# A gated mix of windowed attention and a token MLP: second x block transposed by DMA, its gate logits on VectorE, and a new order for the first microseconds

## The chip, the cores and the metric

The kernel runs on one core of a Trainium2 chip. A core has TensorE (PE: matrix products, with a separate stream of weight loads, PEld), VectorE (DVE), ScalarE (ACT), GpSimd (POOL) and SyncE (SP), which here issues every DMA. The metric is the device time of one execution in microseconds (us), as the median of several runs.

## The reference

```python
def _A_ref(x, wqkv, wo):            # B, S, D = 1, 2048, 512
    H = 32; Dh = D // H; W = 256
    qkv = (x @ wqkv).reshape(B, S, 3, H, Dh).transpose(2, 0, 3, 1, 4)
    q, k, v = qkv[0], qkv[1], qkv[2]
    scores = jnp.einsum("bhqd,bhkd->bhqk", q, k) * (Dh ** -0.5)
    # a query sees its own and the 255 earlier tokens; the others get -1e9
    p = _softmax(scores, axis=-1)
    o = jnp.einsum("bhqk,bhkd->bhqd", p, v)
    return o.transpose(0, 2, 1, 3).reshape(B, S, D) @ wo

def _B_ref(x, w1, b1, w2, b2):      # F = 1376, over the token axis
    h = _layernorm(x, axis=-1)
    u = _gelu(jnp.einsum("bsd,sf->bdf", h, w1) + b1)
    y = jnp.einsum("bdf,fs->bds", u, w2) + b2
    return y.transpose(0, 2, 1)

g = _sigmoid((x * gate_w).sum(-1, keepdims=True))
return g * _A_ref(x, wqkv, wo) + (1 - g) * _B_ref(x, w1, b1, w2, b2)
```

Both parts read the same x (2048 x 512, bf16). Attention has 32 heads of 16 columns and a window of 256 tokens; the MLP mixes tokens, so its first product needs the normalised x of all 2048 tokens before it can be finished.

## The kernel before, in words

x is cut into four blocks of 512 tokens (16 tiles of 128). x is loaded with tokens on the partitions (`xo`, tasks `x0.0`, `x0.2`, `x1.4`, `x2.8`, `x3.12`), for the statistics (`bs`, `ba`: mean and variance), the normalised copy `h` and the gate logits. For the Q, K and V products a transposed copy is needed (`XT0` to `XT3`). Blocks 0 and 1 are transposed on PE from `xo` (tasks `xta0.*`, `xta1`, `xtb1.*`, line 588), into PSUM, and copied out by ACT or DVE (`xtc`, lines 582 and 583). Blocks 2 and 3 are loaded a second time by a transposing DMA (`xt2`, `xt3`, line 444).

The weights of Q and K come as four loads of 128 rows (`wqk0` to `wqk3`, line 451), those of V in one (`wv`, line 455). A projection is a chain of four products over these rows (`q0_1` is part 0 of Q for block 1; `k`, and `v` by token tile, likewise; `q0_1.0` and `q0_1.2` are its first and second two products). For block 0 the first product of a chain is cut into two halves of 256 columns (`.0`, `.1`), so that it can start with half of the block; `.2` to `.4` are the products with weight rows 1 to 3. All products of these chains, and those of the MLP, stand at line 647.

Scores are made per token tile and group of heads (`s3.A0`, `s3.B1`, `s3.CNone`; lines 919 and 899), each into two pairs of PSUM banks; ACT takes their exp (`e`, line 944); POOL or DVE zeroes what is outside the window (`m`, lines 516, 960, 980); PE multiplies with V (`pv`, line 1005); DVE transposes, divides by the sum and transposes back (`n1`, `n2`, `nz`, `n3`, `n4`). Two corner pieces per tile need V rows on other partitions, which SP copies (`vs`, `vz`). The MLP's first product makes eleven chains `u0` to `u10` of 16 products, which need all 16 `h`; one block of gelu steps on ACT follows; then `y0` to `y15`, eleven products of the MLP and four of the output projection in one bank, are scaled and biased by `f` and stored by `o`.

The gate logits: for blocks 0 and 1 PE multiplies XT with the gate vector (`gate0`, `gate1`, 16 products of one column each, line 779). For blocks 2 and 3 DVE multiplies `xo` with a broadcast copy of the vector (`gw`, line 487) and adds up along the row (`gl8` to `gl15`, line 799). `gatem`, `gatee` and `ez` turn them into factors that the division `nz` uses.

The order on each engine is written out by hand in `PLAN` (from line 190), one list of task names per engine; the digits after a colon are the PSUM banks or buffers that a task takes. Each engine works through its list in order, so a task that waits holds everything behind it. `arrange` (line 85) only merges the five lists; the times given to the tasks serve that merge. `THEN` names score and `pv` tasks after which the products that follow are issued as four products of 32 columns each, in the tile shape of `pv`, instead of one of 128. At the start PE multiplies zeros (`warm`, line 571), 7 times.

Of the kernel before, what the change touches and what calls it, by code (L numbers as in the profile page):

```python
# [84 lines left out]
def arrange(tasks):  # L85
# [21 lines left out]
    while len(order) < len(tasks):  # L107
# [84 lines left out]
        warm:6 xta0.1:37 xta0.0:65 k3_0.0:4 k2_0.0:5 k1_0.0:1 k0_0.0:0 k2_0.1 k0_0.1 q0_0.0:3 q1_0.0:2 q1_0.1  # L192
        k2_0.2 q0_0.1 k1_0.1 q1_0.2 k3_0.1 q0_0.2 k0_0.2 k1_0.2 k3_0.2 xta1:67 xtb1.2 xtb1.3 q1_0.3 k1_0.3 xtb1.1
        q1_0.4 k1_0.4 q0_0.3 xtb1.0 q2_0.0:7 q0_0.4 q2_0.1 q2_0.2 k0_0.3 q2_0.3 k0_0.4 k2_0.3 q2_0.4 k2_0.4 k3_0.3
        q3_0.0:6 s0.A0:02 q3_0.1 q3_0.2 q3_0.3 q3_0.4 q0_1.0:5 k3_0.4 q0_1.2 v3.0:7 s1.B0:02 v3.2 v0.0:6 v0.2
        s1.A1:40 v1.0:7 v1.2 k3_2.0:6 k3_2.2 v5.0:5 biast:4 v5.2 v2.0:7 s1.CNone:20 v2.2 s0.CNone:24 gate0:6
        s-1.CNone:02 k3_1.0:6 k3_1.2 k2_2.0:7 s0.A1:02 k2_2.2 q3_1.0:5 q3_1.2 v12.0:6 v12.2 v14.0:7 v14.2 pv-1.0:0
        s2.B1:42 q1_1.0:6 k2_1.0:7 q1_1.2 k2_1.2 s1.A0:04 pv0.0:2 pv0.1 v15.0:7 pv0.2 v15.2 k0_2.0:6 k0_2.2
        s1.B1:04 v6.0:7 v6.2 v10.0:6 v10.2 s2.A0:20 k1_1.0:7 k1_1.2 v4.0:4 v4.2 v13.0:5 v13.2 pv1.0:2 pv1.1 pv1.2
        pv1.3 s2.B0:60 v7.0:4 v7.2 pv1.4 k0_1.0:5 k0_1.2 v8.0:4 v8.2 s2.A1:06 v11.0:5 v11.2 v9.0:4 s2.CNone:02 v9.2  # L200
        q2_1.0:5 k1_2.0:7 k1_2.2 q2_1.2 u2.0:6 s3.A0:02 u3.0:7 u2.2 u3.2 s3.CNone:40 u3.4 u3.6 gate1:3 u2.4 u3.8
        s4.B1:24 pv2.0:0 pv2.1 pv2.2 pv2.3 u2.6 u3.10 s3.B0:42 u3.12 u3.14 u2.8 u2.10 s3.A1:04 u2.12 u2.14 q0_2.0:7
        s3.B1:02 q0_2.2 u7.0:6 u7.2 u7.4 u7.6 s4.B0:40 pv3.0:2 pv3.1 pv3.2 pv3.3 u7.8 u7.10 s4.A0:04 u7.12 q3_2.0:7
        u7.14 s4.A1:20 q3_2.2 u0.0:6 u0.2 s5.B0:24 u0.4 u0.6 u0.8 u10.0:7 s4.CNone:02 u10.2 u10.4 u0.10 s6.B0:40
        u10.6 u0.12 u10.8 u10.10 u10.12 s5.B1:24 pv4.0:0 pv4.1 pv4.2 pv4.3 u0.14 u10.14 s5.A1:24 u6.0:6 u6.2 u6.4
        s6.A0:20 u6.6 q2_2.0:7 q2_2.2 s5.A0:42 u6.8 u6.10 u6.12 u6.14 s5.CNone:04 k3_3.0:7 k3_3.2 u5.0:6 s6.A1:20
        u5.2 q1_2.0:7 u5.4 q1_2.2 u5.6 s6.B1:24 pv5.0:0 pv5.1 pv5.2 pv5.3 u5.8 u5.10 s7.A0:42 u5.12 u1.0:7 u1.2
        s8.B0:04 u5.14 u1.4 u1.6 s6.CNone:02 k1_3.0:6 u1.8 k1_3.2 s7.B0:40 u1.10 u1.12 u4.0:6 u1.14 u4.2
        s7.CNone:24 pv6.0:0 pv6.1 pv6.2 pv6.3 q0_3.0:7 u4.4 s8.CNone:24 u4.6 q0_3.2 u4.8 s8.B1:02 u4.10 u4.12 u4.14
        s7.B1:40 u9.0:7 u9.2 u8.0:6 u9.4 s7.A1:42 u8.2 u9.6 u9.8 s8.A1:04 u8.4 u9.10 pv7.0:2 pv7.1 u9.12 u8.6  # L210
        s8.A0:04 u9.14 u8.8 u8.10 u8.12 u8.14 s9.B0:40 pv7.2 pv7.3 q1_3.0:7 q2_3.0:5 q2_3.2 pv8.0:0 pv8.1 pv8.2
        q1_3.2 k2_3.0:4 q3_3.0:5 pv8.3 q3_3.2 k0_3.0:6 k0_3.2 y0.0:7 y0.2 k2_3.2 y0.4 y0.6 y4.0:6 s9.B1:20 y0.8
        y4.2 y4.4 y0.10 s9.A0:42 y0.11 y0.13 y4.6 s9.CNone:40 y4.8 y4.10 y4.11 y4.13 s9.A1:42 y8.0:7 y8.2 y7.0:6
        y8.4 s10.B1:40 y7.2 y8.6 y7.4 s13.CNone:24 y7.6 y7.8 y8.8 y8.10 y7.10 s11.CNone:20 y7.11 y8.11 y8.13
        s10.A0:42 y7.13 pv9.0:0 pv9.1 pv9.2 s10.CNone:64 pv9.3 y1.0:3 y1.2 y9.0:2 y1.4 s10.B0:64 y9.2 y1.6 y1.8
# [12 lines left out]
        xtc0.0.1 xtc0.1.0 xtc0.1.1 xtc1.2 xtc1.3 xtc1.1 xtc1.0 kc1_0 kc0_0 kc2_0 e0.A0.0:4 e0.A0.1 kc3_0 e1.B0.0:3
        vc3 vc0 e1.A1.0:1 e1.B0.1 e1.A1.1 vc5 e1.CNone.0:2 e1.CNone.1 e0.CNone.0:0 vc2 e-1.CNone.0:5 gatee0
        e-1.CNone.1 e0.CNone.1 kc3_1 e0.A1.0:6 kc2_2 e0.A1.1 vc12 vc14 e2.B1.0:5 e2.B1.1 kc2_1 e1.A0.0:4 e1.A0.1  # L230
        vc15 kc0_2 e1.B1.0:6 vc6 e1.B1.1 e2.A0.0:0 vc10 e2.A0.1 vc4 vc13 e2.B0.0:4 vc7 e2.B0.1 kc0_1 vc8 e2.A1.0:3
        vc11 e2.A1.1 e2.CNone.0:2 e2.CNone.1 vc9 e3.A0.0:1 e3.A0.1 e3.CNone.0:6 e3.CNone.1 e4.B1.0:7 e4.B1.1
        e3.B0.0:0 gatee1 e3.B0.1 e3.A1.0:4 e3.A1.1 e3.B1.0:3 e3.B1.1 e4.B0.0:2 e4.B0.1 gatee2 e4.A0.0:5 e4.A0.1
        e4.A1.0:1 e4.A1.1 e5.B0.0:6 e5.B0.1 e4.CNone.0:0 e4.CNone.1 e6.B0.0:4 e6.B0.1 gatee3 e5.B1.0:3 e5.B1.1 ub0
        e5.A1.0:2 e5.A1.1 e6.A0.0:0 e6.A0.1 e5.A0.0:5 e5.A0.1 e5.CNone.0:1 e5.CNone.1 e6.A1.0:7 e6.A1.1 e6.B1.0:8
        e6.B1.1 e7.A0.0:2 e7.A0.1 e8.B0.0:3 e8.B0.1 e6.CNone.0:6 e6.CNone.1 e7.B0.0:5 e7.B0.1 e7.CNone.0:1
        e7.CNone.1 e8.CNone.0:0 e8.CNone.1 e8.B1.0:4 e8.B1.1 e7.B1.0:6 e7.B1.1 e7.A1.0:8 e7.A1.1 e8.A1.0:7 e8.A1.1
        e8.A0.0:2 e8.A0.1 e9.B0.0:5 e9.B0.1 gelu e9.B1.0:1 e9.B1.1 e9.A0.0:6 e9.A0.1 e9.CNone.0:7 e9.CNone.1
        e9.A1.0:0 e9.A1.1 e10.B1.0:8 e10.B1.1 e13.CNone.0:2 e13.CNone.1 e11.CNone.0:3 e11.CNone.1 e10.A0.0:4
# [42 lines left out]
def kernel(  # L282
# [996 lines left out]
```

## Time and profile before

| | |
|---|---|
| Median of 5 runs | 206.68 us (206.05 to 207.07) |
| Profiled execution: its time / its span | 206.59 us / 204.9 us |
| Busy: PE, PEld | 196.9 us (96%), 93.3 us (46%) |
| Busy: ACT, DVE, POOL | 170.2 us (83%), 149.7 us (73%), 81.5 us (40%) |
| First product with weights starts / first u product | 6.76 us / 49.77 us |
| Two DMA transposes: SP held, first and second | 7.21 us, 3.65 us |

The span runs from the first to the last instruction. In the timeline a line gives the start in us, the length, engine, line, operation, output<-input, shapes and the count of merged instructions; in brackets stands how long the engine was idle before and what it waited for. In the chain of waits each piece is what the end of the kernel was waiting for at that moment. "SPq" is SyncE's queue: an issue there that takes long holds all later loads. "Issue to landing" counts from the issuing instruction to the last part of the data.

### The profile page before, as it was taken

Reading aid. Unit: us, or ns where it says so; the run is one execution under the profiler, and the core shown is the slowest. Engines: PE = TensorE matmul, PEld = TensorE weight load, DVE = VectorE, ACT = ScalarE, POOL = GpSimd, SP = SyncE. Lnnn points to the kernel's source line nnn. Section 1 sums busy time; section 2 is a strip of 40 time slices with the busy share of each in tenths; the row PEclk is TensorE's granted clock in tenths of the full one; section 3 lists DMA queues with packets and bytes.
Section 4 is the critical chain, followed back from the end, with each engine's and each line's share of the span. In section 5 each row is a group of like instructions: output and inputs, shape, how many; then the busy total and the mean of one; then the engine's idle time right before and its main releaser. Section 6 shows DMA issues by size and latency. Waiting matters only on the chain.

```text
span 204.9 us, 8428 instructions
## 1 busy us (share of the span) xinstructions
PE 196.9 (96%) x3768; PEld 93.3 (46%) x3768; DVE 149.7 (73%) x273; ACT 170.2 (83%) x200; POOL 81.5 (40%) x80
## 2 busy tenths in 40 slices
PE   7899999999999999999999999899999999999993
PEld 3453443343635345453544454334445534553662
DVE  3699889998796836689776689463795865758483
ACT  2379999989978898998889697999897889798831
POOL 8722479634425044004072440009974204400930
PEclk9999999999999999999999999999999999999999
DMA  5998997930040101001059890010103031000201
GB/s 160 347 236 185 248 307 227 352 120 11 3 113 24 31 2 31 3 3 28 3 137 410 317 308 3 18 36 10 52 0 96 17 113 56 11 29 3 80 3 53
DMA packets 21106, 21.45 MB, mean 105 GB/s; under 512 B 5486, under 2 KB 19182, under 8 KB 21070
## 3 DMA queue, kind: packets, MB, share of 16 engines
q1 hardware_dynamic: 21070, 20.92, 33.9%
q8 instruction: 29, 0.48, 1.0%
q14 instruction: 7, 0.06, 0.1%
HBM read 15.61 MB, written 2.10 MB: 86 GB/s over the span
## 4 chain that ended last, share of the span: by engine, by line
PE 85%; DVE 6%; DMA 3%; issue 2%; ACT 1%; SPq 1%; DVEq 0%
PE pb L647 61%; PE ps L1005 11%; PE ps L919 9%; DMA xo<-in_A_x_dram 3%; PE ps L899 3%; DVE ps L1083 2%; DVE zt L1100 1%; ACT et L944 1%; DVE ps L1087 1%; SPq L435 1%; PE pb L588 1%; SPq L451 0%; DVE rd L1091 0%; DVE KT L583 0%; DVE ot L422 0%
## 5 line engine op out<-in xcount | busy, mean ns | idle before, releaser
L944 ACT ACTIVATE et<-ps 128x1024 bf16<-128x1024 f32 (+1 forms) x106 | 99.1, 997 | 12.4 <-PE ps L919 8.3
L516 POOL TENSOR_SCALAR_AFFINE_SELECT et<-et 128x1024 bf16<-128x1024 bf16 (+3 forms) x41 | 54.4, 1336 | 68.2 <-ACT et L944 32.9
L944 ACT ACTIVATE XT<-ps 128x1024 bf16<-128x1024 f32 x48 | 46.5, 1028 | 5.2 <-PE ps L919 4.1
L647 PEld LDWEIGHTS <-wb 128*128 128x128 bf16 (+4 forms) x438 | 31.7, 98 | 36.4 <-issue 5.9
L647 PE MATMUL pb<-h,wb 128*128 128x512 bf16 (+1 forms) x176 | 44.3, 381 | 0.0
L647 PE MATMUL pb<-ug,wb 128*128 128x512 bf16 (+6 forms) x262 | 44.3, 367 | 0.0
L647 PE MATMUL pb<-XT,wqkv 128*128 128x512 bf16 (+1 forms) x136 | 32.9, 368 | 0.5 <-DVE XT L583 0.5
L516 POOL TENSOR_SCALAR_AFFINE_SELECT XT<-XT 128x1024 bf16<-128x1024 bf16 x12 | 13.7, 1145 | 44.6 <-ACT XT L944 38.0
L1083 DVE STREAM_TRANSPOSE ps<-ps 128x1024 f32<-128x1024 f32 (+1 forms) x17 | 20.4, 1202 | 14.7 <-PE ps L1005 14.6
L919 PE MATMUL ps<-QZ,KT 32*128 32x256 bf16 (+1 forms) x528 | 23.9, 262 | 1.7 <-ACT et L944 0.8
L1005 PEld LDWEIGHTS <-VA 128*32 128x32 bf16 (+1 forms) x1056 | 19.4, 97 | 6.0 <-issue 3.6
L422 DVE TENSOR_SCALAR ot<-pb,c,c 128x512 bf16<-128x512 f32 (+1 forms) x15 | 11.6, 774 | 14.0 <-PE pb L647 13.8
L731 DVE TENSOR_TENSOR QZ<-pb,par 128x1024 bf16<-128x1024 f32 x16 | 19.3, 1219 | 1.7 <-PE pb L647 1.4
L919 PEld LDWEIGHTS <-KT 32*128 32x128 bf16 x528 | 8.0, 92 | 25.7 <-ACT et L944 12.7
L647 PEld LDWEIGHTS <-wqkv 128*128 128x128 bf16 x136 | 11.6, 98 | 13.6 <-issue 1.4
L1005 PE MATMUL ps<-et,VA 128*32 128x128 bf16 (+2 forms) x752 | 17.4, 216 | 0.0
L647 PE MATMUL pb<-wo,xo 128*128 128x512 bf16 (+2 forms) x98 | 17.0, 371 | 0.0
L647 PE MATMUL pb<-wqkv,XT 128*128 128x512 bf16 x64 | 16.4, 381 | 0.0
L1005 PEld LDWEIGHTS <-VZ 128*32 128x32 bf16 x832 | 13.2, 98 | 0.0
L747 DVE BATCH_NORM_STATS2 stats<-xo 128x6 f32<-128x512 bf16 x16 | 10.6, 683 | 3.4 <-DMA xo<-in_A_x_dram 3.3
L1100 DVE TENSOR_TENSOR zt<-ps,rd 128x512 bf16<-128x512 f32 (+1 forms) x17 | 11.2, 659 | 0.5
L980 DVE TENSOR_TENSOR et<-et,mask 128x1024 bf16<-128x1024 bf16 x13 | 9.9, 764 | 2.2 <-ACT et L944 2.2
(72 smaller groups left out, 181.6 us busy)
## 6 DMA issues: line engine op xcount, KB each, us to landing
wb<-in_B_w_dram SPq DMA_DIRECT2D x8, 512.0 KB, 5.3
wb<-in_B_w_dram SPq DMA_DIRECT2D x2, 2048.0 KB, 10.6
out_dram<-ot SPq DMA_DIRECT2D x15, 128.0 KB, 1.8
VZ<-VA SPq DMA_DIRECT2D x26, 70.0 KB, 2.1
xo<-in_A_x_dram SPq DMA_DIRECT2D x3, 512.0 KB, 5.6
wb<-in_B_w_dram SPq DMA_DIRECT2D x4, 352.0 KB, 7.1
wqkv<-in_A_wqkv_dram SPq DMA_DIRECT2D x4, 256.0 KB, 6.0
wb<-in_B_w_dram SPq DMA_DIRECT2D x1, 1024.0 KB
```

Source lines behind the costliest of these rows:

```text
L422: return nc.vector.tensor_scalar(out=out_, in0=in_, scalar1=scale, scalar2=bias, op0=ALU.mult, op1=ALU.add)
L516: return nc.gpsimd.affine_select(out=out_, in_=in_, pattern=[[0, n] for n in pattern] + [[step, HB]], compare_op=op, fill=0.0, base=base_, ...
L647: made.append(nc.tensor.matmul(buf(b)[c:z_, c0:c0 + w_], lhsT=lhsT[:, c:z_], rhs=rhs, start=(j == 0), stop=(j == n - 1), skip_group_check= ...
L731: lambda k=k, b=b: nc.vector.tensor_tensor(out=QZ[:, k, :, (i % NQ) * SB:(i % NQ + 1) * SB], in0=buf(b)[:, None, :].to_broadcast([P, 2, SB ...
L747: f"bs{t_}", {"DVE": 0.67}, lambda b=b, t_=t_: nc.vector.bn_stats(buf(b)[:], xo[:, t_, :]),
L899: made.append(nc.tensor.matmul(buf(b2[r // 2])[m_:m_ + HB, at:at + P], lhsT=keys(t_, k)[rows, a:a + HB], rhs=q[rows], start=True, stop=Tru ...
L919: made.append(nc.tensor.matmul(to[:, :, done:done + m], lhsT=keys(t_, k)[rows], rhs=q[rows], start=True, stop=True, tile_position=(32 * r, 0),
L944: lambda n_=n_: nc.scalar.activation(out=shape(buf(e)[:, n_ * 1024:(n_ + 1) * 1024]), in_=shape(buf(b2[n_])), func=ACT.Exp, scale=SCALE),
L980: return nc.vector.tensor_tensor(out=view, in0=view, in1=mask[:, "AB".index(x), None, :].to_broadcast([P, n_, HB]), op=ALU.mult)
L1005: return lambda: nc.tensor.matmul(to(), lhsT=v() if callable(v) else v, rhs=buf(e)[rows, col:col + n], start=first, stop=last, tile_positi ...
L1083: f"n1{j}", {"DVE": 0.10 + 0.53 * f_}, lambda: nc.vector.transpose(out=view(), in_=view()), [last], uses=[o],
L1100: lambda: nc.vector.tensor_tensor(out=buf(zt)[:, 0:w].rearrange("q (k b d) -> q k b d", k=4, d=DH), in0=blocks_of()[:, :, :, 0:DH], in1=bu ...
```

## The change

`NPE` goes from 2 to 1: block 1 is no longer transposed on PE but loaded a second time by a transposing DMA (`xt1`). The gate logits get a count of their own, `NGP = 1`, so block 1's come from DVE (`gl4` to `gl7`), and `gate1` is gone. The four loads of Q and K weight rows stand right behind the first x block on SP. Block 0's transposes are cut into four tasks, one per bank, instead of two. There are 5 products with zeros instead of 7. The task `table`, an exp of one column late in ACT's list, is dropped. All five lists of `PLAN` and the set `THEN` are new, and some of the planner's times. No arithmetic changes except where block 1's logits are summed.

```diff
 PLAN = dict(
     PE="""
-        warm:6 xta0.1:37 xta0.0:65 k3_0.0:4 k2_0.0:5 k1_0.0:1 k0_0.0:0 k2_0.1 k0_0.1 q0_0.0:3 q1_0.0:2 q1_0.1
-        k2_0.2 q0_0.1 k1_0.1 q1_0.2 k3_0.1 q0_0.2 k0_0.2 k1_0.2 k3_0.2 xta1:67 xtb1.2 xtb1.3 q1_0.3 k1_0.3 xtb1.1
-        q1_0.4 k1_0.4 q0_0.3 xtb1.0 q2_0.0:7 q0_0.4 q2_0.1 q2_0.2 k0_0.3 q2_0.3 k0_0.4 k2_0.3 q2_0.4 k2_0.4 k3_0.3
-        q3_0.0:6 s0.A0:02 q3_0.1 q3_0.2 q3_0.3 q3_0.4 q0_1.0:5 k3_0.4 q0_1.2 v3.0:7 s1.B0:02 v3.2 v0.0:6 v0.2
...
+        warm:5 xta0.1.0:4 xta0.1.1:3 xta0.0.0:7 xta0.0.1:5 q0_0.0:0 q1_0.0:4 k1_0.0:6 k0_0.0:1 k1_0.1 q1_0.1 q0_0.1
+        k0_0.1 q1_0.2 q2_0.0:2 k0_0.2 k1_0.2 k3_0.0:7 q0_0.2 q1_0.3 k3_0.1 q1_0.4 q0_0.3 k1_0.3 k2_0.0:3 q0_0.4
+        k0_0.3 k1_0.4 q2_0.1 k0_0.4 k3_0.2 k2_0.1 q2_0.2 k3_0.3 k3_0.4 q2_0.3 q2_0.4 s1.A0:04 k2_0.2 k2_0.3
+        q3_0.0:7 k2_0.4 q0_1.0:6 q0_1.2 q3_0.1 q3_0.2 s0.A0:20 q3_0.3 q3_0.4 v0.0:5 v0.2 k3_1.0:4 v1.0:6
+        s-1.CNone:20 k3_1.2 v3.0:5 v1.2 v3.2 s1.B0:02 biast:7 v2.0:4 v2.2 q3_1.0:6 q3_1.2 v14.0:7 s0.A1:02 v14.2
+        v12.0:4 gate0:5 v5.0:6 v5.2 v12.2 s0.CNone:02 k2_2.0:7 k3_2.0:6 k3_2.2 s1.CNone:04 k2_2.2 pv-1.0:2 v10.0:6
...
+        pv7.0:2 u8.14 pv7.1 pv7.2 s9.B0:60 pv7.3 q2_3.0:4 q2_3.2 k0_3.0:7 k2_3.0:5 k0_3.2 q1_3.0:6 k2_3.2 pv8.0:0
+        pv8.1 pv8.2 pv8.3 q3_3.0:7 q1_3.2 y4.0:4 y0.0:5 q3_3.2 y0.2 y4.2 y4.4 y4.6 s9.A0:20 y0.4 y0.6 y0.8 y0.10
+        y0.11 y4.8 s10.B0:26 y0.13 y4.10 y4.11 y4.13 s9.CNone:02 y8.0:5 y8.2 y8.4 s11.CNone:06 y8.6 y7.0:4 y7.2
...
     DVE="""
...
+        zeros bs2:0 ba2 bs0:1 bs3:0 ba3 xtc0.1.1 bs1:0 ba0 parity const ba1 qc1_0 qc0_0 bs8:0 qc2_0 bs11:1 qc0_1
+        qc3_0 gl11 gl10 gl8 ba11 ba8 vc3 biasc bs10:0 bs6:1 qc3_1 ba10 gl4 h0 ba6 bs9:0 bs7:1 ba9 gatem0 bs5:0
...
     POOL="""
-        ident blanks ones pow0 masks m0.A0 m1.B0 m1.A1 m-1.C m0.C m0.A1 m1.C pow2 pow1 m1.A0 m1.B1 pow3 m2.A1 m2.A0
...
+        ident blanks masks ones pow0 m1.A0 m-1.C m0.A1 pow2 m0.A0 m0.C m1.C m1.B0 pow1 m1.B1 m1.A1 pow3 m2.A0 m2.B0
...
     SP="""
-        x0.2 x0.0 wqk0 wqk1 x2.8 x1.4 wqk2 wqk3 gw wv xt2 bias x3.12 xt3 w1_00 vs0 w1_03 w1_01 w1_23 vs1 vs2 w1_13
...
+        x0.2 x0.0 wqk0 wqk1 wqk2 wqk3 x2.8 xt1 wv gw x1.4 bias xt3 vs0 xt2 w1_02 x3.12 vs1 w1_20 w1_13 vz2:0 w1_11
...
-    NPE = 2
+    NPE = 1
+    NGP = 1
...
-    add("table", {"ACT": 1.4}, lambda: nc.scalar.activation(th[:], eps[:, 0:1], ACT.Exp), [k0])
...
-        "warm", {"PE": 2.6}, lambda: warming(7), [kz], takes=[wu], ins=14,
+        "warm", {"PE": 2.2}, lambda: warming(5), [kz], takes=[wu], ins=10,
...
     for n_ in range(2):
-        b2 = [bank("xt"), bank("xt")]
-        t = add(
-            f"xta0.{n_}", {"PE": 0.86},
-            lambda n_=n_, b2=b2: emit_xt(
-                0, b2, [(c, 2 * n_ + t, c % 2 * 256 + t * P) for c in range(4) for t in range(2)]
-            ),
-            [dx[2 * n_], k1], takes=b2, ins=16,
-        )
         for g in range(2):
+            b1 = bank("xt")
+            t = add(
+                f"xta0.{n_}.{g}", {"PE": 0.23 if n_ else 0.43},
+                lambda n_=n_, g=g, b1=b1: emit_xt(
+                    0, {g: b1}, [(2 * g + c, 2 * n_ + t, c * 256 + t * P) for c in range(2) for t in range(2)]
+                ),
+                [dx[2 * n_], k1], takes=[b1], ins=8,
+            )
...
-        if i < NPE:
+        if i < NGP:
             gb = bank("xt")
```

The loops that make block 1's transposes and their copies run over `range(1, NPE)` and so make nothing; `load_t(i)` runs for `i` from `NPE` on and makes `xt1`. Mask multiplies (`m`), copies (`kc`, `vc`, `ub`) and some output steps (`f12`, `f13`) change engines in the new lists: 32 mask multiplies stand with DVE and 44 with POOL, where it was 30 and 46.

## The prediction

> **What bounds the kernel now.** I read the page's busy shares and its chain of waits first, then the timeline of the first 24 us, then the DMA landings, because the diff rewrites the start.
>
> ```profile
> PE 196.9 (96%) x3768; PEld 93.3 (46%) x3768; DVE 149.7 (73%) x273; ACT 170.2 (83%) x200; POOL 81.5 (40%) x80
> ...
> PE 85%; DVE 6%; DMA 3%; issue 2%; ACT 1%; SPq 1%; DVEq 0%
> ```
>
> TensorE is the bound: 8 us idle in 204.9, most of it at the two ends and around the gelu. A plan gains only by giving PE less to do or less to wait for. The timeline shows the start:
>
> ```profile
> 1.38 3.17 PE L571 MATMUL pb<-ug 128*128 128x512 bf16 x7 [1.38 <-DVE ug L498]
> ...
> 4.33 1.91 PE L588 MATMUL pb<-ident,xo 128*128 128x128 bf16 x16
> ...
> 6.62 7.21 SPq L444 DMA_TRANSPOSE XT<-in_A_x_dram  x1
> ...
> 6.65 0.10 PEld L647 LDWEIGHTS <-wqkv 128*128 128x128 bf16 x1 [0.67 <-DMA wqkv<-in_A_wqkv_dram]
> ...
> 6.93 0.33 PEld L647 LDWEIGHTS <-wqkv 128*128 128x128 bf16 x4 [0.19 <-ACT XT L582]
> ...
> 10.37 0.83 PE L588 MATMUL pb<-ident,xo 128*128 128x128 bf16 x12 [0.62 <-DMA xo<-in_A_x_dram]
> ...
> 15.92 3.65 SPq L444 DMA_TRANSPOSE XT<-in_A_x_dram  x1
> ```
>
> Three things: the first product waits for the first weight rows (6.65); PE then stops until the second x block lands (10.37); and a DMA transpose holds SP's queue for 3.65 to 7.21 us. The chain has the gate products of block 1, and the timeline of ACT and of PE the wait after the gelu:
>
> ```profile
> 53.45 0.38 PE pb L779 x16
> ```
> ```profile
> 127.39 1.28 ACT L944 ACT_TABLE_LOAD   x1 [1.30 <-issue]
> ...
> 129.76 0.40 PE L919 MATMUL ps<-QZ,KT 32*128 32x256 bf16 x8 [0.84 <-ACT et L944]
> ```
>
> Issue to landing (min/median/max), of the Q/K weight rows and of the two transposes:
>
> ```profile
> DMA to landing us min/median/max: 4.8/6.0/7.1
> ```
> ```profile
> DMA to landing us min/median/max: 5.6/7.4/9.3
> ```
>
> **The change part by part.** The profiled execution took 206.59 us: span 204.9 and 1.7 around it. The median of the runs is 206.68, 0.09 above, which I neglect.
>
> *Weight rows and x0, the start of PE.* The first two weight rows keep their issue (1.82, 2.32) and land 4.8 us later, at 6.62 and about 7.3. So the first product stays at 6.76, whatever else is early. Two warming products fewer (0.43 each) and finer transposes let PE finish x0 near 5.4 instead of 6.24; this only lengthens the wait, worth 0. It does remove one pause: the fifth product came at 7.42 for a late copy of XT (0.2); now each copy needs four transposes, starts from 4.3 and is through by 6.3. **-0.2.** Rows 2 and 3 are issued at 2.80 and 3.27 instead of 3.82 and 4.37, ahead of 512 KB of x. Row 3 landed at 11.5 behind 1 MB of x; x1.4, issued at 3.27, landed 7.0 us later (10.3), and 256 KB take 0.7 at the 350 GB/s of those microseconds: rows 2 and 3 land near 8.0 and 8.7. By the new order PE asks for them at 8.7 and 9.0 (eight halves of 0.108, then a mixture of halves and 0.216s): tight, 0 to 0.3 lost, in the remainder below.
>
> *Second block off PE.* 16 transposes go: twelve start within 0.67, so 0.056 each: **-0.9.** The stop for x1.4 goes (9.59, the end of the last product, to 10.37): **-0.8.** Nobody else waits early for x1.4: its statistics and logits stand behind 17 us of DVE's queue. ACT loses four XT copies (0.60 each).
>
> *What replaces it: xt1 on SP.* Issued eighth, at about 4.4. It holds SP and everything behind: wv, gw, x1.4, four bias loads, xt3. From the rows: SP held 3.65 to 7.21, free between 8.0 and 11.6; landing 5.6 to 9.3 after issue, 10.0 to 13.7. I take SP free at 10.1 and landing at 12.1, since x2.8 ahead of it ends near 10.1 and both transposes landed about 2 us after SP came free (13.83 to 15.9; 19.57 to 21.5). PE first needs it for q0_1: from 6.76, eight chains of 0.86 less the parts ordered later, and one score step of 0.43, give 13.3. Hidden, by 1.2; at the worst end 0.4 is lost. wv is issued at 10.1; the load behind the second transpose landed after 4.4, wv itself took 7.8 behind 2 MB. I take 14.5, for the queue is then as empty as behind the second transpose; PE asks at 15.4. Hidden, 0.9 to spare; at 11.6 + 4.4 = 16.0, 0.6 is lost. The V products also need POOL's ones, now behind the masks: blanks end at 4.5, masks 2.6, ones 2.9: 10.0. xt3 lands near 18 (asked near 21.6). vs0 holds SP until the first V copy, about 18; then xt2, 5.6 to landing: 24.7, asked near 26. The w1 loads behind start some 3 us later; DMA was idle half of 31 to 33 and ended at 42.5, u starts at 48. Hidden too.
>
> *Gate of block 1.* 16 PE products, **-0.4**; instead four DVE steps of 0.77 (684 + 81 ns), 3.1 us on an engine 73% busy. Ahead of the last h, which the u products need, DVE has less: five logits, the five steps of output 1 and two copies leave that stretch, two logits, four copies and one Q product enter it: 47.2 to 44.3 by the rows' means. So u is not held. DVE also gains two mask multiplies (0.69 each) that POOL loses.
>
> *The plan's remainder.* Reading both orders with the code's modes, PE changes tile shape 177 times instead of 179; scores after products cost 0.1 by the trace's starts: **-0.2.** 68 product pairs instead of 18 run as column tiles; one such pair (8 instructions) spans 0.44 against 0.43: 0.5 in all, taken into the last term. After the gelu, ACT loads its table only when s9's scores are there, and the next score step needs bank pair 2 back. Before, 1.7 us of products cover 1.28 + 1.03 (wait 0.84); the new order puts 2.4 between s9.A0 and s10.B0, so 0.2 to 0.3 is left: **-0.6.** The table task near the end (0.20 on ACT, in a gap of 0.74) is worth 0. The last products follow pv15.2 as before: y15r.11 comes 2.5 after it in both.
>
> *Unknown: new waits in a rearranged order.* Between 17 and 119 us PE has five waits of 0.25 to 0.4 for ACT and DVE. Low end: they vanish, -0.8. High end: as many again, the tiles' 0.5 and the bounds of wv and xt1, +1.6. I take **+0.4**, one more such wait, because the new order still meets ACT's 0.97 load in this stage:
>
> ```profile
> 17.00:50.00 33.00, 32.55 (x472) 13.49 (x470) 30.66 (x80) 31.83 (x48) 18.48 (x19) 1.00 0.79 223
> ```
>
> (columns: PE, PEld, DVE, ACT, POOL). ACT's first exp moves from 15.2 to about 12.7 and it copies less, so its lead is as large as PE's.
>
> Sum: -0.2 - 0.9 - 0.8 - 0.4 - 0.2 - 0.6 + 0.4 = -2.7; 206.6 - 2.7 = **203.9 us**. Own range: 202.7 (waits gone) to 205.4 (gelu gain lost, wv and xt1 at their worst ends).
>
> **The rivals.**
>
> *The clock comes late.* The first transposes start 0.107 apart, the later ones 0.056; products of 256 columns at 6.76 take 0.108: full clock came between 5.93 and 6.76, 4.6 to 5.4 us after the first warming product, with one hole of 0.5. Now there are holes near 3.5 (0.15) and from 5.4 to 6.76. If that time must be earned again from 3.65, full clock comes at 8.2 to 9.0, and half speed from 6.76 costs 0.7 to 1.1; from 6.76 on, 2.3 to 2.7. I price it 1.6: 205.5, still faster. For it: 1.4 us without work. Against it: before, the clock rose across a stretch that ended in such a hole.
>
> [...]
>
> *V weights late: slower.* wv queues behind xt1 on SP. With SP free at 11.6 and wv's own 7.8, it lands at 19.4; PE, in order, stands at v0 from 15.4: 4.0 lost, 207.9. It decides from a landing at 18.1 on. For it: both durations are rows of this trace. Against: the 7.8 had 2 MB ahead.
>
> *The front's gain is hidden anyway.* ACT at 31.8 of 33 us could set the pace to 50 us; then -1.9 and -0.6 fall away, leaving 206.6 - 0.6 + 0.4 = 206.4, the same. Against: ACT itself starts earlier.
>
> **How the numbers follow.** Forecast 0.58, late clock 0.13, hidden 0.12, late V weights 0.17 (with it a late xt2 or row, to the same effect). About what a measurement can tell from no change is 0.3%, 0.6 us. Faster: 0.58 + 0.13 = 0.71; same 0.12; slower 0.17. The range runs from 202.7 to 206.9, just past the hidden case; outside it lie the late weights (0.17) and little below.
>
> **What would show it.** Right: first product at 6.7 to 6.8; Q/K products without a stop to 12; first exp near 12.7; xt1 landing before 13.3 and wv before 15.4; the first u at 47 to 48 instead of 49.8; the wait after the gelu under 0.4. Wrong: 256-column products 0.21 apart after 6.76; PE waiting for XT or wqkv DMA between 13 and 17, or for XT near 26; a first u at 49 or later; scores waiting for ACT or DVE more than 3 us in all.

## The result and the profile after

The changed kernel takes **208.26 us** in the median (206.54 to 209.79, 24 runs) where the kernel before, run beside it, takes 206.4 (205.84 to 207.35, 43 runs): ratio 1.0075, 95% interval 1.0059 to 1.0091. It is slower by 1.9 us where 2.7 us less were predicted, and its runs spread over 3.3 us instead of 1.5. Ratios here and below leave out executions over 1.5% above their kernel's fastest and those at a lower granted clock; medians are of all executions. Its profiled execution took 206.54 us (span 204.8), the lowest of its runs; what it shows are the losses that even the best execution has.

Page of the changed kernel, busy times, the chain of waits by engine, and the queue on which instructions are fetched (packets, MB, share of 16 DMA engines' time):

```profile
PE 195.1 (95%) x4015; PEld 92.8 (45%) x4015; DVE 150.8 (74%) x283; ACT 168.8 (82%) x195; POOL 80.5 (39%) x78
...
q8 instruction: 31, 0.51, 1.1%
...
PE 46%; DVE 5%; POOL 3%; ACT 2%; DMA 2%; issue 2%; DVEq 0%; SPq 0%; POOLq 0%; ACTq 0%
```

The shares of the chain sum to some 60%, because it could be followed back to 80 us only; they are not to be set beside the 85% of before. PE does 1.8 us less work, in an unchanged span. Its matrix instructions rose from 3768 to 4015 (a product run as four column tiles counts four times), its instruction packets from 29 to 31. The start, in the timeline of the changed kernel:

```profile
3.68 1.67 PE L586 MATMUL pb<-ident,xo 128*128 128x128 bf16 x16
...
4.23 5.21 SPq L443 DMA_TRANSPOSE XT<-in_A_x_dram  x1
...
6.29 5.59 PE L645 MATMUL pb<-XT,wqkv 128*128 128x256 bf16 x32 [0.94 <-ACT XT L580]
...
12.26 1.02 ACT L942 ACTIVATE et<-ps 128x1024 bf16<-128x1024 f32 x1 [0.18 <-PE ps L917]
...
47.78 1.89 PE L645 MATMUL pb<-h,wb 128*128 128x512 bf16 x8
```

The first u product in the timeline of the kernel before:

```profile
49.77 0.59 PE L647 MATMUL pb<-h,wb 128*128 128x512 bf16 x2
```

Here everything came as predicted or better: 32 products without a stop, first exp at 12.26 instead of 15.2, and the first u product at 47.78 instead of 49.77. **A lead of 2.0 us is there at 48 us.** The windows after that, first of the changed kernel, then of the kernel before (columns: window, length, then busy time and instructions of PE, PEld, DVE, ACT, POOL, then PE's granted clock, DMA share, GB/s):

```profile
50.00:119.00 69.00, 66.76 (x1519) 31.98 (x1520) 52.69 (x92) 58.52 (x66) 31.11 (x22) 1.00 0.27 92
119.00:130.00 11.00, 11.00 (x185) 5.27 (x183) 10.26 (x22) 9.80 (x10) 0.00 (x0) 1.00 0.08 22
130.00:205.00 75.00, 70.06 (x1749) 34.80 (x1747) 46.48 (x68) 59.43 (x65) 21.13 (x16) 1.00 0.14 41
```
```profile
50.00:119.00 69.00, 68.30 (x1416) 32.16 (x1415) 50.42 (x83) 60.22 (x68) 22.47 (x19) 1.00 0.26 86
119.00:130.00 11.00, 10.02 (x179) 4.63 (x177) 8.92 (x13) 9.66 (x9) 2.24 (x2) 1.00 0.36 121
130.00:205.00 75.00, 71.52 (x1623) 35.07 (x1615) 47.73 (x73) 60.16 (x66) 28.50 (x20) 1.00 0.13 39
```

Between 50 and 119 us PE works 1.5 us less than before in the same time: new waits. From 119 to 130 it gains 1.0: the wait after the gelu is gone. From 130 on it works 1.5 us less, and yet ends at the same moment. So 2.0 - 1.5 + 1.0 - 1.5 leaves nothing.

The largest new wait is in the chain of waits near 91 us (start, length, what):

```profile
84.12 1.00 DVE et L978
...
85.27 2.13 POOL et L516
...
87.45 2.13 POOL et L516
...
89.64 1.49 POOL XT L516
...
91.17 0.86 PE ps L1003 x63
```

Three mask multiplies in a row on POOL, behind a DVE that was late, hold `pv5` for 1.13 us. The loss after 130 us looks different:

```profile
161.64 1.19 PE ps L1003 x108
162.83 0.70 issue
163.53 0.36 PE ps L1003 x20
```

In the middle of 128 products that depend on nothing new, PE stands still (0.92 between the starts), with no wait that the profile shows; at 197.21 again, 0.51. In what follows the length of a stop is the time from product start to product start. The kernel before has no such stop in its profile. The question for the experiments is what these are, and whether they take the rest in the executions above 206.54.

### The profile page after: what moved, and what is told of

Its sections match the earlier page's. It is cut to its first block, busy times and chain, and to the rows that moved or that the text cites. A ratio compares the mean times of both kernels' runs of the same rounds, so it can differ in the third digit from the quotient of the medians.

```text
span 204.8 us, 8916 instructions
## 1 busy us (share of the span) xinstructions
PE 195.1 (95%) x4015; PEld 92.8 (45%) x4015; DVE 150.8 (74%) x283; ACT 168.8 (82%) x195; POOL 80.5 (39%) x78
## 4 chain that ended last, share of the span: by engine, by line
PE 46%; DVE 5%; POOL 3%; ACT 2%; DMA 2%; issue 2%; DVEq 0%; SPq 0%; POOLq 0%; ACTq 0%
PE pb L645 32%; PE ps L1003 7%; PE ps L917 6%; POOL et L516 2%; DVE ps L1081 2%; DMA out_dram<-ot 2%; PE ps L897 2%; ACT et L942 1%; DVE ug L420 1%; POOL XT L516 1%; DVE zt L1098 1%; DVE ps L1085 1%; ACT XT L942 1%; DVE et L978 0%; ACT ot L418 0%
## 5 line engine op out<-in xcount | busy, mean ns | idle before, releaser
L516 POOL TENSOR_SCALAR_AFFINE_SELECT et<-et 128x1024 bf16<-128x1024 bf16 (+3 forms) x35 | 44.8, 1287 | 71.3 <-ACT et L942 44.8
L942 ACT ACTIVATE XT<-ps 128x1024 bf16<-128x1024 f32 (+1 forms) x48 | 44.8, 988 | 6.0 <-PE ps L897 2.9
L645 PEld LDWEIGHTS <-wb 128*32 128x32 bf16 (+4 forms) x695 | 32.3, 97 | 35.4 <-issue 5.5
L645 PE MATMUL pb<-ug,wb 128*32 128x512 bf16 (+5 forms) x397 | 45.0, 370 | 0.0
L645 PE MATMUL pb<-h,wb 128*32 128x512 bf16 (+2 forms) x298 | 44.5, 381 | 0.0
L516 POOL TENSOR_SCALAR_AFFINE_SELECT XT<-XT 128x1024 bf16<-128x1024 bf16 (+2 forms) x16 | 22.5, 1411 | 37.9 <-ACT XT L942 33.7
L645 PE MATMUL pb<-XT,wqkv 128*128 128x512 bf16 (+2 forms) x154 | 32.4, 369 | 0.9 <-ACT XT L580 0.9
L1003 PE MATMUL ps<-et,VA 128*32 128x128 bf16 (+2 forms) x752 | 19.5, 217 | 0.3 <-issue 0.3
L645 PEld LDWEIGHTS <-wqkv 128*128 128x128 bf16 (+1 forms) x154 | 12.0, 97 | 14.1 <-issue 1.5
L1116 DVE STREAM_TRANSPOSE xo<-zt 128x512 bf16<-128x512 bf16 (+1 forms) x17 | 11.4, 671 | 0.2
```

The source lines that it names most:

```text
L516: return nc.gpsimd.affine_select(out=out_, in_=in_, pattern=[[0, n] for n in pattern] + [[step, HB]], compare_op=op, fill=0.0, base=base_, ...
L645: made.append(nc.tensor.matmul(buf(b)[c:z_, c0:c0 + w_], lhsT=lhsT[:, c:z_], rhs=rhs, start=(j == 0), stop=(j == n - 1), skip_group_check= ...
L942: lambda n_=n_: nc.scalar.activation(out=shape(buf(e)[:, n_ * 1024:(n_ + 1) * 1024]), in_=shape(buf(b2[n_])), func=ACT.Exp, scale=SCALE),
L1003: return lambda: nc.tensor.matmul(to(), lhsT=v() if callable(v) else v, rhs=buf(e)[rows, col:col + n], start=first, stop=last, tile_positi ...
L1116: return nc.vector.transpose(out=to, in_=src)
```

## The experiments

The kernel before ran beside each of them: 206.43 to 206.55 in the median.

### The same kernel again, and the clock

Theory then: in most executions TensorE's full clock comes late, as the first rival had it. Runs: the changed kernel again (`after_again`); the changed kernel with seven warming products (`after_warm7`); the kernel before with five (`before_warm5`).

```diff
-        "warm", {"PE": 2.2}, lambda: warming(5), [kz], takes=[wu], ins=10,
+        "warm", {"PE": 2.2}, lambda: warming(7), [kz], takes=[wu], ins=14,
```

> The changed kernel once more, unaltered, for a second profile: the first one (206.54 us) lies at the lower edge of its own runs (206.5 to 209.8, median 208.26). Clock theory: where this profile is slower than 204.8 us of span, the clock record starts later than 4.99 us and the 256-column products after 6.3 us run 0.21 apart, 1 to 2 us lost there. Fetch theory: the clock starts as before, and the extra time stands in PE gaps inside pv groups and in late instruction packets after 60 us (0.86 and 0.48 us such gaps in the first profile). Time 208.2 in either.

> The changed kernel with 7 products of zeros instead of 5. Clock theory: the early hole shrinks, runs narrow to about 206.5 to 207.3 and the median falls by 1.2 to 1.8, to about 206.7. Fetch theory: nothing changes, 208.0 to 208.6 with the same spread.

> The kernel before with 5 products of zeros instead of 7, all else as it was. Clock theory: the holes before the first product grow from 0.5 to about 0.9 us, some runs get the clock late, median 206.8 to 207.6 and a spread of 2 us or more. Fetch theory: 206.4, spread as before (1.5 us).

Measured: 207.41 (206.94 to 209.02, five runs; ratio 1.0069, 1.0039 to 1.0099), 207.02 (205.64 to 208.41; 1.0026, 1.0003 to 1.005) and 206.9 (206.05 to 207.49; 1.0021, 1.0006 to 1.0035). In all three profiles the clock's record begins at 4.4 to 5.6 us, before the first product, and no product of 256 columns starts 0.21 after the one before it. So the clock was not what these executions lost by. The first lost 0.5 us before its first product (6.81 instead of 6.29, the weight rows), the third 0.88 before its first exp (the second x block let PE start at 11.25 instead of 10.37), which stays to its end. There are stops without a wait in both profiles of the changed kernel: at 99.13 (0.45) and 164.03 (0.96) in the first, at 98.89 (0.43), 122.45 (1.09) and 164.46 (0.67) in the second, the slowest of its runs (208.41). Part of them are other stops than in the first profile, in an unaltered kernel too.

The medians do not speak for the fetch theory: with seven warming products the changed kernel's fell by some 1.2 us (0.4 against its five runs beside them) and with five that of the kernel before rose by 0.5, as the clock theory had forecast, where the fetch theory forecast no change. Since the runs also move PE's stream by two product pairs, they do not separate the two.

### The front alone

```diff
-    NPE = 2
+    NPE = 1
+    NGP = 2
...
-        x0.2 x0.0 wqk0 wqk1 x2.8 x1.4 wqk2 wqk3 gw wv xt2 bias x3.12 xt3 w1_00 vs0 w1_03 w1_01 w1_23 vs1 vs2 w1_13
+        x0.2 x0.0 wqk0 wqk1 wqk2 wqk3 x2.8 xt1 wv gw x1.4 bias xt2 x3.12 xt3 w1_00 vs0 w1_03 w1_01 w1_23 vs1 vs2 w1_13
```

`before_front`: the kernel before with block 1 transposed by DMA and the Q and K rows ahead; its gate products stay on PE, and DVE's steps on x1 move behind four Q copies.

> The kernel before with the change's first part alone: second block by DMA transpose, Q and K weight rows behind the first x block, no PE transposes or XT copies of that block; its gate products stay on PE, 7 products of zeros, and the order of the rest is the old one (only the statistics of x1 and x2 move behind the first Q steps on VectorE). If the front's gain of 1.9 us is real and what loses time is the new order of the rest: 204.6 to 205.2. If the gain is lost whatever follows (hidden by ScalarE or VectorE): 206.0 to 206.6.

Measured: 207.15 (206.32 to 210.92), ratio 1.0035 (1.0019 to 1.0052). The first exp comes at 14.15 instead of 15.2, but scores then wait for DVE (0.60 at 13.71), which is at the statistics of x1 and x2, and at the 23rd exp that writes `et` (48.22 in the kernel before) 0.14 of the lead is left; a stop without a wait at 164.07 (0.77) takes more than that. So 204.6 to 205.2 was missed. In the old order the front's lead is not passed on; in the new order it is. Where the lead is spent is a matter of the rest of the plan.

### More and fewer column tiles

Theory: PE stops because its instructions come late. In the trace a packet of 16 KB (31 of them, 0.51 MB) starts 2.2 to 2.9 us ahead of each stop's end, and column tiles are what makes the stream dense (24 matrix instructions in 1.41 us at 102.75, where 6 take 1.40 at 95.60). Ten names out of `THEN` in the changed kernel (`after_trim`, 35 pairs of tiled products fewer), ten added in the kernel before (`before_tiles`, 41 pairs more); order and shape changes stay.

```diff
 THEN = set("""
+    s5.A0 s7.A0 s7.A1 s7.B0 s8.A0 s9.B1 s10.B0 s11.A0 s12.A0 s14.B1
```

> The changed kernel with ten names taken out of THEN (s5.A0 s7.A0 s7.A1 s7.B0 s8.A1 s9.B1 s10.A0 s11.A0 s12.B0 s14.B1), which make products in tiles of 32 columns without saving a change of tile shape: 35 pairs of products go back to whole ones, some 400 PE instructions fewer, 177 changes of shape as before. Fetch theory (PE runs out of fetched instructions in the dense pv groups): the gaps of 0.4 to 0.9 us inside pv that end 2.3 to 2.7 us after an instruction packet shrink to one or none, median 206.2 to 207.0, 1 to 1.5 under the changed kernel, and a narrower spread. Masks theory (GpSimd's masks hold PE near 90 us): unchanged, 207.4 to 208.3. Clock theory: unchanged.

> The kernel before with ten such names put into its THEN (s5.A0 s7.A0 s7.A1 s7.B0 s8.A0 s9.B1 s10.B0 s11.A0 s12.A0 s14.B1): 41 pairs of products in tiles of 32 columns, some 490 PE instructions more, the same order and the same number of shape changes. Fetch theory: gaps inside pv appear that were not there, median 207.0 to 208.5, a spread of 2 us or more. Every other theory: 206.4 to 206.8.

Measured: 208.86 (208.18 to 210.57), ratio 1.0122 (1.0093 to 1.015), where less was expected; and 209.04 (208.38 to 210.62), ratio 1.0133 (1.0105 to 1.0161), slower as expected, and by more than the 207.0 to 208.5 forecast. In `before_tiles` PE stands in mid-`pv`, as the chain of waits has it:

```profile
101.14 1.30 PE ps L1006 x106
102.43 0.83 issue
103.26 0.46 PE ps L1006 x16
```

Adding tiles to the kernel before made stops of 1.05 at 103.26 and 1.06 at 179.70. But taking tiles away made stops too, 1.50 at 164.53 and 0.80 at 186.64. So it is not how many instructions there are. It is where in the stream they stand: counted by weight loads (twice, for each product's two instructions) and semaphore instructions, PE's instruction at the end of a stop has these numbers:

```
kernel          stop ends   stands   instruction   remainder by 256   packet: start, length
after             163.53     0.92       6082             194            160.89  1.38
after             197.21     0.51       7873             193            194.76  0.88
after_trim        164.53     1.50       5826             194            161.82  1.21
after_trim        186.64     0.80       6850             194            184.29  0.99
before_tiles      103.26     1.05       3521             193            100.92  0.92
before_tiles      179.70     1.06       6849             193            176.99  1.37
before_front      164.07     0.77       5826             194            161.74  0.96
```

The remainder is the same at places of different plans, with different work standing there. What counts is that it is the same, not its value: the count begins at the program's first instruction in the profile. Such a place, one every 256 instructions, is called a mark below, and the 256 instructions between two marks a block. Of all traces of this study, every stop over 0.4 us at full clock without a wait, 36 of them, ends at remainder 193 or 194, and 1.16 to 1.57 us after the end of an instruction packet. If a packet holds what stands between two marks, an instruction has 64 bytes (16384 by 256), an estimate from these two figures.

### The mask near 91 us

```diff
-        ub6 m5.B0 qc2_2 n43 kc3_3 n44 m6.A1 gatem2 n15 n25 nz5:0 n35:1 n45 ub1 ub5 n16 n26 nz6:1 n36:0 kc1_3 ub4
+        ub6 m5.B0 m5.C qc2_2 n43 kc3_3 n44 m6.A1 gatem2 n15 n25 nz5:0 n35:1 n45 ub1 ub5 n16 n26 nz6:1 n36:0 kc1_3 ub4
...
```

`m5.C` goes from POOL to DVE, in the changed kernel as it is (`after_m5c`) and with the ten names out (`after_trim_m5c`).

> The changed kernel with one mask multiply, m5.C, on VectorE instead of GpSimd (behind m5.B0). Masks theory: GpSimd's three multiplies in a row before 91 us (2.13, 2.13, 1.49) become one, the wait of 1.1 inside pv5 at 90 goes, and 0.8 to 1.1 us are gained at the end: 206.4 to 207.2. Fetch theory: the wait goes and the time is mostly lost again to fetch gaps; 207.2 to 208.0.

> Both edits together. If fetch gaps and the mask wait are what ate the front's gain: 205.0 to 206.0, faster than the kernel before (206.4). If the front's gain is lost elsewhere: 206.4 or more.

Measured: 207.52 (206.59 to 208.97), ratio 1.0066 (1.0037 to 1.0096), and 209.28 (208.35 to 210.52, and one execution of 647.13), ratio 1.0132 (1.0104 to 1.0161). The wait of 1.13 at 91 us is gone, but scores at 87.6 now wait 1.3. Measured by the lag of the exps behind those of the changed kernel's profile, 0.17 is won between 83 and 96 us; the unchanged kernel run again wins 0.26 there, so no gain by the move is to be seen. The wait was real, and the next one stands behind it: DVE, which gave POOL its work late, is now late itself.

### Moving the stream and nothing else

This tells the theories apart. The warming products at the start, in idle time, are cut into more and smaller ones. Plan, waits and work stay; all later instructions stand some pairs further along: 48 or 5 in the kernel before (`before_shift48`, `before_shift5`), 7 or 40 in the changed one (`after_shift7`, `after_shift40`).

```diff
     def warming(n):
-        return [nc.tensor.matmul(buf(wu)[:], lhsT=zeros[:, 0:P], rhs=zeros, start=True, stop=True) for _ in range(n)]
+        return [
+            nc.tensor.matmul(buf(wu)[:, 0:c], lhsT=zeros[:, 0:P], rhs=zeros[:, 0:c], start=True, stop=True)
+            for c in n
+        ]
...
-        "warm", {"PE": 2.6}, lambda: warming(7), [kz], takes=[wu], ins=14,
+        "warm", {"PE": 2.6}, lambda: warming([512] * 1 + [56] * 54), [kz], takes=[wu], ins=110,
```

> The kernel before with nothing changed but its warming: one product of 512 columns and 54 of 56 columns in place of seven of 512, in the idle time ahead of x. That moves every later instruction of PE 48 product pairs further along PE's instruction stream and leaves plan, waits and work as they are. Fetch theory: PE's instructions come in packets of 16 KB, one about every 128 pairs, each asked for when the block before it begins, and PE stands still where a block is used up in less than about 2.9 us. By the starts in the profile of before, with the block edges moved by 48 pairs, seven blocks last under 2.5 us (ending near 78.6, 92.8, 103.0, 144.0, 156.1, 183.4 and 194.3 us) where at its own place none does; the shortfalls sum to 5.1 us at 2.5 us a fetch and 7.9 at 2.9. Expected 210.5 to 215, with stops of 0.5 to 1.5 us of PE at such places. Rival, that a plan's waits or the clock took the gain: a shift of the stream alone changes nothing, 206.2 to 206.9.

> The kernel before with its stream moved by 5 pairs (six products of 512 columns and six of 80 in place of seven of 512). Fetch theory: its shortest blocks, 2.73 and 3.02 us, grow above 3.4; it had no stop in its profile, so 206.0 to 206.5, with a narrower spread. Rival: the same 206.4.

> The changed kernel with its stream moved by 7 pairs (four products of 512 columns and eight of 64 in place of five of 512). Fetch theory: its two blocks of 2.2 and 2.5 us, which the stops near 163 and 197 us follow, grow above 3.4, and the stops go; left is the fetch that waits behind the loads of 103 to 121 us (a stop near 122 of 0 to 1.5 us in some executions). The profiled execution less its two stops is 206.54 - 0.86 - 0.48 = 205.2; expected 205.2 to 206.6, at or under the kernel before. Rival, that waits or the clock took the gain: 207.0 to 208.3, as the unchanged kernel.

> The changed kernel with its stream moved by 40 pairs (45 products of 56 columns in place of five of 512). Fetch theory: eight blocks under 2.9 us (ending near 66.7, 77.7, 99.9, 122.5, 144.6, 157.1, 177.1 and 186.7), shortfalls of 3.0 us at 2.5 us a fetch and 5.6 at 2.9: 208.5 to 212. Rival: no change against the unchanged kernel, 207.0 to 208.3.

Measured: **214.85** (213.82 to 217.59), ratio 1.0413 (1.0373 to 1.0453), for the kernel before moved by 48 pairs, and **212.86** (211.91 to 213.72), ratio 1.0301 (1.0281 to 1.0322), for the changed kernel moved by 40 (208.5 to 212 was forecast). No plan, wait or data transfer was touched. The chain of the first near its end:

```profile
187.61 1.32 PE ps L1008 x122
188.93 1.20 issue
190.13 0.24 PE ps L1008 x6
...
199.40 1.36 PE ps L1008 x128
200.76 0.64 PE pb L650 x14
201.40 1.12 issue
202.52 0.29 PE pb L650 x2
```

Seven places had been worked out from the trace of before; stops came at six of them, at 93.43, 104.69, 148.60, 161.50, 190.13 and 202.52 (times shifted by the stops ahead of them), not at 78.6, and one more at 125.69 (1.91 us). At 78.6 the block of 256 instructions lasted 1.6 us, but its packet had started at 75.87, 1.0 us ahead of the mark at which the block begins. The seven stops sum to 8.7 us, the median rose by 8.4. The exps run 0.1 us ahead of those of the kernel before up to 91 us and 8.1 behind at 203, and each larger step stands at one of the stops. So the place of PE's instructions costs time by itself, and most of the places can be worked out beforehand.

In the trace of the changed kernel moved by 40 pairs the longest stop, 2.38 us to 126.73, is followed by 3.4 us at half the granted clock (126.80 to 130.21; products of 512 columns start 0.43 apart instead of 0.22), which makes it dearer still. No run tests what sets that off.

The small shifts are less clean. The changed kernel moved by 7 pairs takes 207.21 (204.81 to 208.56), ratio 0.9996 (0.9968 to 1.0024). The median of all twelve executions, the slowest at 207.92 to 208.56 among them, is 0.7 above that of the kernel before, 1.05 below the 208.26 of the unmoved kernel and 0.2 below its 207.41 in five more runs. That is within the spread, so a gain in the median is not shown, though single executions are 1.7 below the unmoved kernel's best; the 206.6 at most that was expected was missed. In its trace stops of 0.72 (98.50) and 0.71 (163.05) are left: the blocks ahead of them last 3.3 and 3.5 us without the stop, so 2.9 us for a fetch was too low a bound. The kernel before moved by 5 pairs takes 207.0 (206.35 to 207.72), ratio 1.0026 (1.001 to 1.0043): a miss, 0.5 slower where no change was expected; its trace has no stop over 0.4, only exps that fall behind by 0.27 near 106, 0.13 near 160 and 0.12 near 165 us.

### A store, more warming, and all together

In the trace of the 7-pair kernel scores near 169 us stand 1.26 us. The chain there:

```profile
165.94 0.12 SPq L707
166.06 0.05 issue
166.11 1.97 DMA out_dram<-ot
...
168.18 0.82 DVE ot L421
169.00 0.14 issue
169.14 0.40 PE ps L920 x8
```

SP held the copies for `vz14` 1.97 us instead of 0.54, the store `o1` behind them was late, DVE waited for its buffer, PE for DVE. The unshifted kernel with seven warming products had the same stop at 170.25; the changed kernel's own profile does not. The store, ready long before, is put earlier on SP, in the kernel moved by 7 pairs (`after_shift7_o1`) and in one moved by 10 (`after_shift10_o1`):

```diff
-        w2_1 w2_2 o0 vz9:2 o7 o4 o2 vz12:1 o8 vz11:2 vz13:0 vz14:2 o1 o9 o5 o3 o10 o6 o12 o13 o11 o14 o15r o15l
+        w2_1 w2_2 o0 vz9:2 o7 o4 o2 vz12:1 o8 o1 vz11:2 vz13:0 vz14:2 o9 o5 o3 o10 o6 o12 o13 o11 o14 o15r o15l
```

> The changed kernel with its stream moved by 7 pairs as before, and on SP's queue the store o1 ahead of the copies vz11, vz13 and vz14 instead of behind them. In the trace of the 7-pair shift alone a second copy for vz14 held the queue for 1.97 us instead of 0.54, o1 behind it was issued at 166.11, DVE waited for its buffer until 168.11, and scores at 169.03 stood 1.26 us. Theory that this store is the second wait: that stop goes (in the executions that had it), the store lands by 158, the slowest executions come down; median 206.0 to 206.9, fastest as before near 204.8. Rival, that the spread from 204.8 to 208.6 is the fetch's alone: median unchanged at 207.2, the stop near 169 gone but the time as it was.

> The same with 10 pairs in place of 7 (eleven products of 48 columns and four of 512). By the block lengths worked out from the trace, the block that ends near 116 us, under the loads of 103 to 121, has 6.2 us in place of 5.7, the others over 3.3. Theory that the fetches behind those loads set the rest of the spread: 0.2 to 0.5 under the 7-pair kernel. Rival: the same within 0.3.

Measured: 206.48 (205.21 to 209.12, and one execution of 314.56 at a mean granted clock of 0.562, which is the profiled one and is not read), ratio 0.9984 (0.9956 to 1.0012), and 206.72 (204.58 to 208.06), ratio 0.9992 (0.9966 to 1.0018). The medians lie 0.7 and 0.5 below the kernel without and inside the 206.0 to 206.9 that the theory of the store had, but the executions spread over 3.5 to 3.9 us, the slowest ones did not come down, and so the gain is not shown. Three pairs more of shift make no difference that can be told. The profile of the second shows the first rival of the prediction at work: the clock's record begins at 10.05 us. PE's products from 6 to 8 us, in this kernel and in the changed one:

```profile
6.00:8.00 2.00, 1.37 (x7) 1.00 (x8) 1.33 (x9) 0.29 (x1) 1.84 (x5) 1.00 0.98 343
```
```profile
6.00:8.00 2.00, 1.71 (x13) 1.26 (x14) 1.30 (x9) 0.25 (x1) 1.84 (x5) 1.00 1.01 349
```

Seven products instead of thirteen, 0.21 apart, and the first exp at 14.26 instead of 12.26. Of these 2.0 us, 0.33 is a later first product (6.62 instead of 6.29) and 1.67 the way from there to the first exp. (The window's granted clock says 1.00 in both: it does not cover the time ahead of its record; the starts do.) So the last kernels have seven full warming products and five small ones, the shift of 7 pairs and the early store (`after_best`); the second has `m5.C` on DVE too (`after_best_m5c`).

> The changed kernel with three things put right together: its stream moved by 7 pairs, the store o1 early on SP, and warming of seven products of 512 columns (and five of 64) in place of five, since in the trace of the 10-pair kernel the clock's record began only at 10.05 us and ten 256-column products started 0.21 apart instead of 0.11, first exp 14.26 instead of 12.26. Theory that fetch, store and late clock were what took the lead: median 205.2 to 206.2, no execution over 207.5. Rival, that seven warm products only push the transposes back (they end near 5.9 instead of 5.1, first weight rows 6.2 to 6.6) or that the rest of the spread is something else: 206.5 to 206.9 as the kernels with 5 warm products and the early store.

> The same, with the mask multiply m5.C on VectorE behind m5.B0 in place of GpSimd (the wait of 1.13 us near 91). In the unshifted kernel that move brought the exps at 96 us 0.2 us earlier. Expected 0.1 to 0.3 under the one without; rival: no difference or slower, because VectorE then is late for the next one.

Measured: 206.4 (205.41 to 207.31), ratio 0.9991 (0.9971 to 1.0011): the same median as with five warming products, not the 205.2 to 206.2 expected, though the highest run is lower. Whether that is the clock stays open; in the two profiles its record begins at 6.20 and 7.12 us, no earlier than in the kernel with five. With the mask moved: **205.89** (205.28 to 206.64), ratio 0.9968 (0.9954 to 0.9983). This is the fastest version of the study, 0.7 us under the kernel before and 2.4 under the changed kernel. That the mask gives the 0.5 between the two is not shown: in their profiles the difference is the stop at 122.73 (1.37), which the first has and the second has not. Its trace still has scores that start at 87.94 after 1.19 us without work, and stops that end at 98.98 (0.45) and 163.83:

```profile
161.92 1.12 PE ps L1006 x101
163.04 0.79 issue
163.83 0.44 PE ps L1006 x27
```

## Why the prediction was wrong, point by point

**What bounds the kernel** was read rightly (PE), but "a plan gains only by giving PE less to do or less to wait for" left out a third thing, PE's instructions themselves. The profile of before has their packets in its list of queues, and the kernel's planner carries constants named `BLOCK`, `AHEAD` and `FETCH` (255, 80 and 3.5, assumptions of the planner that no run tests); the prediction used neither. The line of that list, from the page of the kernel before:

```profile
q8 instruction: 29, 0.48, 1.0%
```

**Weight rows, second block, xt1, gate (-0.2, -0.9, -0.8, -0.4): right.** Weight rows landed at 6.24, not 6.62, so the first product came at 6.29. SP was held 5.21, xt1 landed at 11.4 to 11.6 (12.1 taken), wv at 13.5 (14.5), and no product waited for either. The first u came at 47.78, inside 47 to 48. The rivals "hidden anyway" and "V weights late" failed here: the lead came, and the slower end has another mechanism.

**The gelu (-0.6): right**, and larger: 1.0, the whole wait.

**Shape changes and tiles:** 35 pairs of tiled products fewer brought the exps near 111 us forward by at most 0.4, so 0.5 for 50 pairs more was not too low for their time. But it was a price of time only. Each such product is eight instructions instead of two; that they move and thicken the stream was not priced at all.

**"Unknown: new waits" (+0.4): the term that was mis-sized.** It measured 1.5 from 50 to 119 us, inside its own bound of +1.6. (The upper end of the prediction's own range is 205.5 by its terms, not 205.4: 203.9 and 0.6 for the gelu, 0.6 for wv, 0.4 for xt1.) I had argued from ACT's load before 50 us, and that stage was clean; the waits came where POOL's masks queue up (POOL busy 31.1 us of 69 instead of 22.5). I had seen two multiplies move from POOL to DVE in number, and not that POOL's work moved into this stage.

**The step that failed** is the sum itself, which takes a lead at 48 us as a lead at the end and has no term for fetching. Stops without a wait cost 0.92 + 0.51 us in the changed kernel's best execution. That and the waits explain this execution: 206.59 - 2.0 + 1.5 - 1.0 + 1.4 = 206.5, measured 206.54. The median is another 1.7 above. For that I have no trace of the slower executions themselves. The nearest is the one of 208.41 us with seven warming products: its exps are 0.1 behind those of the changed kernel's profile at the start, 0.3 at 101 us, 1.2 at 129 (the stop at 122.45) and 1.75 at 171 (scores that wait for the store). What traces of nearly the same plan show is 0.4 to 0.7 at 99 us, 1.1 to 1.4 at 122, 1.0 to 1.3 at 170 (the store), 0.5 at the start (weight rows landing later) and 1.7 there (the clock), each in some executions and not in others. Moving the stream, the store, the warming and the mask took 2.4 us off the median (208.26 to 205.89, beside 206.4 and 206.55 of the kernel before); how that splits is not shown, since the single steps lie within the spread of the executions.

**Where a packet stops PE and where not:** all 36 stops stand at the same remainder by 256, and 312 of 399 packets start within 1.6 us of the mark ahead of theirs (those after 45 us and outside the loads of 101 to 121). No stop over 0.4 us was found where a block lasts over some 4 us and no large load is in flight. In the kernel moved by 48 pairs PE stood 0.6 to 1.4 us at six of the seven crossings where it uses the block up in 1.5 to 2.4.

**Late clock (rival, 1.6 us):** absent in the changed kernel's profile (record from 4.99 us), present in the profiled execution of `after_shift10_o1` (record from 10.05), at 1.7 us, with products of 256 columns 0.21 apart. The price was near. That holes in the work at the start bring it about was my estimate and is not shown, and neither is that the median comes from it.

## What to carry to other kernels

Where PE is the bound and its stream is dense, count its instructions: mark every 256th, read from the trace how long PE takes from mark to mark, and treat a stretch under some 4 us (256 and 4 us are the figures of this case) as a possible stop of the difference, and a longer one too while loads are in flight. Any edit that adds or drops instructions ahead of such a stretch moves all later marks, so a change at the start can gain 2 us there (2.0 at 48 us in the changed kernel) and lose as much or more later (8.4 in the kernel moved by 48 pairs); before judging it, move the stream by a few dummy products in idle time and measure again. A lead is worth at the end only what the next late engine and the next late packet leave of it: here nothing of 2.0 us.

## What the runs showed of the hardware

- The kernel before, moved by 48 product pairs and otherwise unchanged, is 8.4 us slower: the largest effect of the study comes from where instructions stand.
- A fetch of 16 KB took 0.88 to 1.44 us on the DMA engine in the 36 stops, and PE went on 1.16 to 1.57 us after its end, 2.2 to 2.9 us after its start.
- Most packets (312 of 399 after 45 us, those from 101 to 121 us not counted) start within 1.6 us of PE's passing the mark ahead of theirs. While the weight loads of the second MLP product were in flight (issued at 101.3, 105.5 and 114.2 us in the changed kernel) it was 2.7 to 4.1 us. The mark that PE passes at 116 us separates the executions: with the packet 2.7 to 2.9 us after it (the changed kernel twice, `after_shift7`, `after_best_m5c`) no stop over 0.4 follows at 121 us, with 3.6 to 3.8 (`after_warm7`, `after_m5c`, `after_best`) one of 1.1 to 1.4 does. That the loads delay the packets is read from these starts and was not tested by itself.
- The clock's record began at 4.4 to 7.4 us in all the profiles at full clock but one (6.33 in the kernel before, 4.99 in the changed one), and there (`after_shift10_o1`) at 10.05, with nearly the same warming as in `after_shift7`, where it began at 4.78; what decides it stays open.
